# Sixteen distances between the experts' weights and the operands they meet, one for each expert and inner block

## The chip, the cores and the metric

The kernel runs on one core of one Trainium2 chip, in one launch. The metric is device microseconds. The kernel before was timed in 3 runs: median 689.16 us, lowest 688.44, highest 694.27.

## What is computed

Three layers follow each other. An attention over 2 batches of 8 heads (576 positions, head dimension 64) adds a banded softmax and a softmax over positions averaged by four. Its output is read as x with 1152 rows of 512. Then:

```python
h = x @ w_in                                  # 512 -> 2048
x = (h * (1.0 / (1.0 + np.exp(-h)))) @ w_out  # 2048 -> 512

p = domain_probs / (domain_probs.sum(-1, keepdims=True) + 1e-09)
out = np.zeros((N, D), dtype=np.float32)
for e in range(E):                            # 4 experts, 512 -> 1024 -> 512
    h = np.maximum(x @ w1[e], 0.0)
    out += p[:, e:e + 1] * (h @ w2[e])
```

All is float32. The change touches the place in memory of w1 and w2 alone.

## The kernel before

**Split products.** A float32 operand of the two feed-forward layers is held as a high part and a low part (float32r), and each product is three matmuls: high by high, high by low, low by high (`mm3`, line 493, and `prod`, line 692). In a matmul one operand is stationary (128 columns are loaded into the array by a weight load of its own, PEld in the profile) and the other is moving (256, 320 or 384 columns are streamed through).

**Stages of the experts.** For each expert `e` (4), each chunk of rows `ci` (0 to 2 of 256 rows, 3 of 384) and each inner block `k` (4) there is one stage. `first_products` (line 646) makes 24 matmuls at line 495: w1 stationary, x moving, 256 columns, or 384 in chunk 3. `second_products` (line 703) makes 21 matmuls at line 699: the activations `h` stationary, w2 moving, 256 columns; in chunk 3 another 12 with the tiles `o`, 33 in all. The second products of a stage come after the first products of the next one. This makes 3,072 matmuls for the experts, 192 for each pair of an expert and an inner block in each of the two products: 96 first ones (72 of 256 columns and 24 of 384) and 96 second ones.

**Where the operands lie.** In the built program `xh` and `xl` begin at byte 128 modulo 512 in every partition, `wbuf` at 192, `wext` (and `u5`) at 448, the tiles `h` and `o` at 384. Slices of them begin at multiples of 512 from there, but for the two row chunks of the first feed-forward pass that start at rows 576 and 832 (256 more, modulo 512). "Distance" is here the first byte of the moving operand minus that of the stationary one, modulo 512, which gives before:

| products | moving | stationary | distance |
|---|---|---|---|
| experts, first | `xh`, `xl` | w1 in `wbuf` | 448 |
| experts, second, k = 0, 1 | w2 in `wext` | `h`, `o` | 64 |
| experts, second, k = 2, 3 | w2 in `wbuf` | `h`, `o` | 320 |
| feed-forward, weights in `wext`, `u5` | `xh`, `xl` | w_in | 192 |

**Refilling.** While chunk 3 of an expert runs, the next expert's weights are split into the same places: `split_u` (line 601; ACT writes the high part at line 608, POOL or DVE the low part at line 610) and `split_kk` (line 614; lines 624 and 626). The raw weights come by DMA from SP's queue (line 583) well before. The tile framework makes a write wait for the matmuls that still read the bytes it overwrites, and its scheduler sets each engine's order by the priorities of the ticks (`at_prio`).

Of the kernel before, what the change touches and what calls it, by code (L numbers as in the profile page):

```python
# [9 lines left out]
F32 = mybir.dt.float32  # L10
F32R = mybir.dt.float32r
# [4 lines left out]
ACTF = mybir.ActivationFunctionType  # L16
ALU = mybir.AluOpType
# [16 lines left out]
UW = 2048  # L34
NE = 4
KF = 7 * 256
# [20 lines left out]
STAGE = 4  # L57
EXPERT = 72


@with_exitstack
def attention_moe_kernel(ctx, tc, kqa, kqb, qtl, va, vb, w64, w1d, w2d, dpr, out):
    nc = tc.nc
    PE, ACT, DVE, POOL, SP = nc.tensor, nc.scalar, nc.vector, nc.gpsimd, nc.sync

    const = ctx.enter_context(tc.tile_pool(name="const", bufs=1))
# [22 lines left out]
    xl = const.tile([128, HP, NT], F32R, name="xl")  # L89
    acc = const.tile([128, 9 * 512], F32, name="acc")  # L90
    const.tile([128, 16], F32, name="gap")
    wbuf = const.tile([128, 8 * UW], F32R, name="wbuf")
    const.tile([128, 16], F32, name="gap_w")
    prt = const.tile([128, 9, NE + 1], F32, name="pr")
    pr, prs = prt[:, :, 0:NE], prt[:, :, NE:NE + 1]
# [26 lines left out]
    def follow(i, earlier, reason):  # L122
        tc.add_manual_dep(i.ins, earlier.ins.name, mybir.DependencyInfo(mybir.DependencyClass.NoSync, mybir.DependencyReason.DATA),
                          reason=reason)

    def behind(eng, i):
        if eng in latest:
            follow(i, latest[eng], "background work")
        return i
# [7 lines left out]
    unit = {}  # L137
    wext = []
# [3 lines left out]
    def slot(u):  # L142
        s = SLOT[u] if u < 8 else (2, 3)[u % 2]
        if s == 5:
            wext.append(u5_p[0].enter_context(tc.tile_pool(name="u5", bufs=1)).tile([128, 2 * UW], F32R, name="u5"))
        t, o = (wext[s - 4], 0) if s > 3 else (wbuf, 2 * UW * s)
        return t[:, o:o + UW], t[:, o + UW:o + 2 * UW]
# [23 lines left out]
    def split_piece():  # L171
        u, j, t = loaded.popleft()
        with at_prio(needed(u, j) - LEAD_SPLIT):
            split_raw(u, j, t)
        held[0] -= 1
        load_piece()

    def split_raw(u, j, t):
        if j == 0:
            unit[u] = slot(u)  # L180
        h, l = unit[u]
        if u < 8:
            c = slice(j * 512, (j + 1) * 512)
            v = t.bitcast(I32).rearrange("p (n t) -> p n t", t=2)
            a = d_p.tile([128, 512], F32, tag="dec", name="dec")
            ai = a.bitcast(I32)

            top = t.bitcast(U16).rearrange("p (n t) -> p n t", t=4)[:, :, 1]
            ACT.activation(out=a, in_=v[:, :, 1].bitcast(F32), func=ACTF.Copy, scale=2.0 ** -112)
            ACT.activation(out=v[:, :, 0], in_=top, func=ACTF.Copy, scale=2.0 ** -13, bias=2.0 ** -14 - 0.5)  # L190
            i = DVE.scalar_tensor_tensor(out=ai, in0=ai, scalar=3, in1=v[:, :, 0],  # L191
                                         op0=ALU.logical_shift_left, op1=ALU.bitwise_or)
            if u in behind_job:
                follow(i, behind_job[u], "first weights")
            DVE.scalar_tensor_tensor(out=ai, in0=v[:, :, 1], scalar=-2 ** 31, in1=ai,  # L195
                                     op0=ALU.bitwise_and, op1=ALU.bitwise_or)
            ACT.activation(out=h[:, c], in_=a, func=ACTF.Copy)  # L197
            POOL.tensor_tensor(out=l[:, c], in0=a, in1=h[:, c].bitcast(F32), op=ALU.subtract)  # L198
        else:
            c = slice(j * 1024, (j + 1) * 1024)  # L200
            behind(ACT, ACT.activation(out=h[:, c], in_=t, func=ACTF.Copy))
            behind(DVE, DVE.tensor_tensor(out=l[:, c], in0=t, in1=h[:, c].bitcast(F32), op=ALU.subtract))


    actx = ExitStack()
# [279 lines left out]
    def attn_tick():  # L485
        for _, _, f, args in sorted(plan.pop(tick[0], ()), key=lambda e: e[:2]):
            prio(tick[0] - (0 if f in main_parts else LEAD_ATTN))
            f(*args)
        tick[0] += 1
        prio(tick[0])  # L490
# [66 lines left out]
    wk, w1k = {}, {}  # L557

    def tick_of(e, ci, k):
        return 96 + EXPERT * e + STAGE * (4 * ci + k) + (2 * k if ci == 3 else 0)  # L560
# [12 lines left out]
    def stage_ahead():  # L573
        while todo and not pieces:
            i = next((i for i, p in enumerate(stg_pools) if held[i] < 3), None)
            if i is None:
                break
            held[i] += 1
            e, x, k = todo.popleft()
            t = stg_pools[i].tile([128, 1024], F32, tag="stg", name="kst")  # L580
            staged[e, x, k] = (t, i)
            with at_prio(need_of(e, x, k) - LEAD_KLOAD):
                SP.dma_start(out=t.rearrange("p (s c) -> p s c", c=256) if x == "k" else t,
                             in_=w2d[e, k] if x == "k" else w1d[e, :, 1024 * k:1024 * k + 1024])
# [10 lines left out]
                                (c[:, 0], t[:, 2], c[:, 2]), (c[:, 1], t[:, 1], c[:, 0])):  # L595
                    behind(eng, eng.tensor_tensor(out=o, in0=a, in1=b, op=ALU.subtract))

    def home_u(k):
        h, l = slot(8 + k // 2)
        c = slice(1024 * (k % 2), 1024 * (k % 2) + 1024)  # L600
        return h[:, c], l[:, c]

    def split_u(e, k):
        t, i = staged.pop((e, "u", k))
        h, l = w1k[k] = home_u(k)
        for c in (slice(0, 512), slice(512, 1024)):
            with at_prio(tick_of(e, 0, k) - LEAD_USPLIT):
                ACT.activation(out=h[:, c], in_=t[:, c], func=ACTF.Copy)
                eng = POOL if k in U_LO_POOL else DVE
                eng.tensor_tensor(out=l[:, c], in0=t[:, c], in1=h[:, c].bitcast(F32), op=ALU.subtract)  # L610
        held[i] -= 1
        stage_ahead()

    def split_kk(e, k):
        t, i = staged.pop((e, "k", k))
        t = t.rearrange("p (s c) -> p s c", c=256)
        c = sums.pop((e, "k", k))
        b, o = (wext[0], 2 * KF * k) if k < 2 else (wbuf, 2 * UW * (k - 2))
        h = b[:, o:o + KF].rearrange("p (s c) -> p s c", c=256)
        l = b[:, o + KF:o + 2 * KF].rearrange("p (s c) -> p s c", c=256)  # L620
        parts = (slice(2, 4), slice(4, 6), slice(0, 2), slice(6, 7))
        for part, (r, x) in enumerate(zip(parts, (t[:, 0:2], t[:, 2:4], c[:, 0:2], c[:, 2:3]))):
            with at_prio(tick_of(e, 0, k) + 6 - LEAD_KSPLIT):
                a = ACT.activation(out=h[:, r], in_=x, func=ACTF.Copy)  # L624
                eng = POOL if (k, part) in LO_ON_POOL else DVE
                b = eng.tensor_tensor(out=l[:, r], in0=x, in1=h[:, r].bitcast(F32), op=ALU.subtract)  # L626
                if e == 0 and k > 1:
                    behind(ACT, a)
                    behind(eng, b)
        wk[k] = (h, l)  # L630
        held[i] -= 1
        stage_ahead()
# [165 lines left out]
    def close_attn():  # L798
        while plan:
            attn_tick()  # L800
        actx.close()
        late = ctx.enter_context(tc.tile_pool(name="late", bufs=1))
        wext.append(late.tile([128, 4 * KF], F32R, name="wext"))
        u5_p.append(ExitStack())
        pp_p.append(ctx.enter_context(tc.tile_pool(name="pp", bufs=1, space=PSUM)))

# [6 lines left out]
    for hf in range(2):  # L813
        u0 = 4 * hf
        dt = 48 / (12 * len(CHUNKS[hf]))
        for ci, (o, n) in enumerate(CHUNKS[hf]):
# [15 lines left out]
            if hf == 0 and ci == 2:  # L832
                close_attn()
                limit[0] = 6
            if hf == 1 and lastc:
                u5_p[0].close()
                ks_p.append(ctx.enter_context(tc.tile_pool(name="ks", bufs=2)))
                stage_ahead()
                for k in range(4):
                    sum_ahead(0, k)  # L840
                    if k < 2:
                        split_kk(0, k)
# [26 lines left out]
    for k in range(2, 4):  # L869
        split_kk(0, k)  # L870
    for k in range(4):
        w1k[k] = home_u(k)

    class Chunk:
        pass
# [1 line left out]
    def finish(st, ch, p):  # L877
        e, ci, k = st.at
        prio(p)
        second_products(st, ch)  # L880
        if ci == 3 and e < NE - 1:
            split_kk(e + 1, k)
            if k < 2:
                sum_ahead(e + 1, k + 2)
        if k == 3:
            outputs(e, ci, ch, p)

    before = None
    for e in range(NE):
        for ci in range(4):  # L890
            ch = Chunk()
            for k in range(4):
                st = Stage()
                st.at = (e, ci, k)
                first_products(st)
                if ci == 3 and e < NE - 1:
                    split_u(e + 1, k)
                if ci == 2 and k % 2 == 0 and e < NE - 1:
                    sum_ahead(e + 1, k // 2)
                if before:  # L900
                    finish(*before, tick_of(e, ci, k) + (3 if ci == 3 else 2))
                before = (st, ch)
# [57 lines left out]
```

## Time and profile before

| | us |
|---|---|
| median of 3 runs | 689.16 |
| lowest and highest run | 688.44, 694.27 |
| profiled execution, first to last instruction (span) | 693.6 |
| TensorE matmul busy | 659.5 (95%) |
| VectorE, ScalarE, GpSimd busy | 440.3, 332.0, 247.5 |

The profile lists no time of its own for the profiled execution beside its span. Busy time of PE is the union of its matmuls, which overlap in the pipeline: a matmul of 256 columns is shown with some 280 ns although the next one starts 113 to 118 ns later. The pace, start to start, is therefore read from how many matmuls fill a stretch.

### The profile page before, as it was taken

Reading aid. Unit: us, or ns where it says so; the run is one execution under the profiler, and the core shown is the slowest. Engines: PE = TensorE matmul, PEld = TensorE weight load, DVE = VectorE, ACT = ScalarE, POOL = GpSimd, SP = SyncE. Lnnn points to the kernel's source line nnn. Section 1 sums busy time; section 2 is a strip of 40 time slices with the busy share of each in tenths; the row PEclk is TensorE's granted clock in tenths of the full one; section 3 lists DMA queues with packets and bytes.
Section 4 is the critical chain, followed back from the end, with each engine's and each line's share of the span. In section 5 each row is a group of like instructions: output and inputs, shape, how many; then the busy total and the mean of one; then the engine's idle time right before and its main releaser. Section 6 shows DMA issues by size and latency. Waiting matters only on the chain.

```text
span 693.6 us, 13797 instructions
## 1 busy us (share of the span) xinstructions
PE 659.5 (95%) x5516; PEld 641.9 (93%) x5516; DVE 440.3 (63%) x882; ACT 332.0 (48%) x753; POOL 247.5 (36%) x346
## 2 busy tenths in 40 slices
PE   4779779999999999999999999999999999999996
PEld 3659669999999999999999999999999999999996
DVE  4678967638664643675665985548855669756444
ACT  4559766647653532544335643345533356433321
POOL 4344762114240000344264432456232654322210
PEclk9597989999999999999999999999999999999999
DMA  8665663105250210042001420004300010000001
GB/s 248 215 183 166 184 176 96 34 1 161 92 174 1 81 44 1 1 144 70 1 1 48 136 61 1 1 2 122 93 31 1 1 60 3 1 32 17 17 31 45
DMA packets 16927, 48.16 MB, mean 69 GB/s; under 512 B 2976, under 2 KB 4256, under 8 KB 16864
## 3 DMA queue, kind: packets, MB, share of 16 engines
q1 hardware_dynamic: 16864, 47.29, 22.0%
q8 instruction: 43, 0.70, 0.4%
q14 instruction: 20, 0.16, 0.1%
HBM read 44.93 MB, written 2.36 MB: 68 GB/s over the span
## 4 chain that ended last, share of the span: by engine, by line
PE 83%; DMA 6%; DVE 6%; ACT 2%; issue 2%; POOL 1%; SPq 0%; ACTq 0%; DVEq 0%; POOLq 0%
PE mm L495 53%; PE p L699 26%; DMA stg<-in_w_dram 3%; DMA vg<-in_va_dram 2%; DVE dec L191 1%; DVE dec L195 1%; DVE gl L521 1%; PE s L328 1%; PE o L420 1%; PE t L388 1%; PE o L416 1%; DVE acc L727 1%; DVE gf L515 0%; POOL vg L265 0%; PE s L352 0%
## 5 line engine op out<-in xcount | busy, mean ns | idle before, releaser
L495 PE MATMUL mm<-xh,wbuf 128*128 128x256 f32 (+2 forms) x1280 | 268.7, 296 | 3.4 <-ACT xh L432 2.6
L495 PEld LDWEIGHTS mm<-xh,wbuf 128*128 128x128 f32 x1280 | 211.0, 190 | 4.7 <-ACT xh L432 3.0
L495 PE MATMUL mm<-xl,wbuf 128*128 128x256 f32 (+2 forms) x640 | 189.8, 297 | 0.0
L681 POOL TENSOR_TENSOR r<-r 128x128 f32<-128x128 f32 x160 | 93.5, 597 | 183.2 <-ACT r L675 143.7
L684 DVE TENSOR_TENSOR h<-r,h 128x384 fp32r<-128x384 f32 (+1 forms) x128 | 91.4, 717 | 64.6 <-ACT h L683 64.4
L495 PEld LDWEIGHTS mm<-xl,wbuf 128*128 128x128 f32 x640 | 121.6, 190 | 0.1
L683 ACT ACTIVATE h<-r 128x384 fp32r<-128x384 f32 (+1 forms) x128 | 73.2, 577 | 85.3 <-POOL r L681 54.1
L495 PE MATMUL mm<-gh,wbuf 128*128 128x256 f32 (+2 forms) x512 | 106.0, 300 | 6.4 <-ACT wbuf L197 3.5
L699 PE MATMUL p<-wext,h 128*128 128x256 f32 x672 | 91.5, 279 | 0.0
L495 PEld LDWEIGHTS mm<-gh,wbuf 128*128 128x128 f32 x512 | 83.8, 191 | 8.0 <-ACT wbuf L197 3.7
L699 PE MATMUL p<-wbuf,h 128*128 128x256 f32 x672 | 84.5, 278 | 0.0
L699 PEld LDWEIGHTS p<-wext,h 128*128 128x128 f32 x672 | 84.4, 188 | 0.0
L699 PEld LDWEIGHTS p<-wbuf,h 128*128 128x128 f32 x672 | 81.2, 188 | 0.0
L495 PE MATMUL mm<-gl,wbuf 128*128 128x256 f32 (+2 forms) x256 | 74.7, 296 | 0.5 <-DVE gl L521 0.5
L675 ACT ACTIVATE r<-mm 128x512 f32<-128x512 f32 x48 | 28.7, 597 | 75.5 <-PE mm L495 75.1
L681 DVE TENSOR_TENSOR r<-r 128x128 f32<-128x128 f32 x96 | 33.5, 349 | 37.7 <-ACT r L675 33.0
L495 PEld LDWEIGHTS mm<-gl,wbuf 128*128 128x128 f32 x256 | 48.6, 190 | 0.8 <-DVE gl L521 0.8
L521 DVE TENSOR_TENSOR gl<-gf,gh 128x256 fp32r<-128x256 f32 (+2 forms) x64 | 34.8, 547 | 18.0 <-ACT gh L520 15.4
L198 POOL TENSOR_TENSOR wbuf<-dec,wbuf 128x512 fp32r<-128x512 f32 x24 | 32.5, 1360 | 31.1 <-ACT wbuf L197 20.2
L727 DVE SCALAR_TENSOR_TENSOR acc<-p,pr,acc 128x256 f32<-128x256 f32 (+1 forms) x63 | 36.1, 605 | 5.9 <-PE p L699 5.9
L626 POOL TENSOR_TENSOR wext<-kst,wext 128x512 fp32r<-128x512 f32 x8 | 10.7, 1344 | 78.4 <-ACT wext L624 42.9
L515 DVE SCALAR_TENSOR_TENSOR gf<-th,mm 128x256 f32<-128x256 f32 (+2 forms) x64 | 28.4, 449 | 15.3 <-ACT th L514 13.6
(122 smaller groups left out, 980.2 us busy)
## 6 DMA issues: line engine op xcount, KB each, us to landing
stg<-in_w_dram SPq DMA_DIRECT2D x32, 512.0 KB, 4.3
kst<-in_w2d_dram SPq DMA_DIRECT2D x16, 512.0 KB, 3.6
kst<-in_w1d_dram SPq DMA_DIRECT2D x12, 512.0 KB, 3.6
kq<-in_kqa_dram SPq DMA_DIRECT2D x8, 419.0 KB, 3.3
kq<-in_kqb_dram SPq DMA_DIRECT2D x8, 323.0 KB, 10.8
vg<-in_va_dram SPq DMA_DIRECT2D x8, 288.0 KB
stg<-in_w1d_dram SPq DMA_DIRECT2D x4, 512.0 KB
vw<-in_vb_dram SPq DMA_DIRECT2D x8, 180.0 KB
```

Source lines behind the costliest of these rows:

```text
L191: i = DVE.scalar_tensor_tensor(out=ai, in0=ai, scalar=3, in1=v[:, :, 0], op0=ALU.logical_shift_left, op1=ALU.bitwise_or)
L198: POOL.tensor_tensor(out=l[:, c], in0=a, in1=h[:, c].bitcast(F32), op=ALU.subtract)
L495: ins = [PE.matmul(out=ps, lhsT=l, rhs=r, start=(first and i == 0), stop=(last and i == n - 1)) for i, (l, r) in enumerate(pairs)]
L515: DVE.scalar_tensor_tensor(out=gf[:, 0:n], in0=th[:, 0:n], scalar=1.0, in1=ps[:, 0:n], op0=ALU.add, op1=ALU.mult)
L521: latest[DVE] = DVE.tensor_tensor(out=gl[ft][:, 0:n], in0=gf[:, 0:n], in1=gh[ft][:, 0:n].bitcast(F32), op=ALU.subtract)
L626: b = eng.tensor_tensor(out=l[:, r], in0=x, in1=h[:, r].bitcast(F32), op=ALU.subtract)
L675: ACT.activation(out=r[:, 0:4].rearrange("p s t -> p (s t)"), in_=ps[:, 0:512], func=ACTF.Relu)
L681: latest[eng] = eng.tensor_tensor(out=r[:, o], in0=r[:, a], in1=r[:, b], op=op)
L683: ACT.activation(out=h, in_=r[:, part], func=ACTF.Copy)
L684: latest[DVE] = DVE.tensor_tensor(out=l, in0=r[:, part], in1=h.bitcast(F32), op=ALU.subtract)
L699: ins = [PE.matmul(out=ps, lhsT=x, rhs=y, start=(opens and k == 0 and i == 0), stop=(k == 3 and i == n - 1), skip_group_check=True) for i, ...
L727: DVE.scalar_tensor_tensor(out=o, in0=ps, scalar=p, in1=o, op0=ALU.mult, op1=ALU.add)
```

## The change

The first weights `w1` of each expert and inner block are moved by a number of bytes that gives their first products one of 16 distances, and `w2` likewise for the second products (`GAPS`, picked by `ROW_W1` and `ROW_W2`). `home_u` now lays the high and low halves of one inner block side by side with 128 floats to spare, `split_raw` uses `home_u` for the first expert's w1, and `wbuf` and `wext` grow by 2048 and 1024 bytes, both multiples of 512. Each value stands once in each table; the distances are now:

| expert | first products, k = 0 to 3 | second products, k = 0 to 3 |
|---|---|---|
| 0 | 448, 0, 256, 64 | 320, 64, 448, 0 |
| 1 | 480, 32, 320, 96 | 32, 464, 128, 384 |
| 2 | 464, 16, 384, 128 | 496, 256, 48, 96 |
| 3 | 496, 48, 416, 192 | 192, 416, 16, 480 |

```diff
+GAPS = (0, 16, 32, 48, 64, 96, 128, 192, 256, 320, 384, 416, 448, 464, 480, 496)
+ROW_W1 = ((12, 0, 8, 4), (14, 2, 9, 5), (13, 1, 10, 6), (15, 3, 11, 7))
+ROW_W2 = ((9, 4, 12, 0), (2, 13, 6, 10), (15, 8, 3, 5), (7, 11, 1, 14))
...
-    wbuf = const.tile([128, 8 * UW], F32R, name="wbuf")
+    wbuf = const.tile([128, 8 * UW + 512], F32R, name="wbuf")
...
     def split_raw(u, j, t):
-        if j == 0:
+        if j == 0 and u < 8:
             unit[u] = slot(u)
-        h, l = unit[u]
         if u < 8:
+            h, l = unit[u]
...
         else:
-            c = slice(j * 1024, (j + 1) * 1024)
-            behind(ACT, ACT.activation(out=h[:, c], in_=t, func=ACTF.Copy))
-            behind(DVE, DVE.tensor_tensor(out=l[:, c], in0=t, in1=h[:, c].bitcast(F32), op=ALU.subtract))
+            h, l = home_u(0, 2 * (u - 8) + j)
+            behind(ACT, ACT.activation(out=h, in_=t, func=ACTF.Copy))
+            behind(DVE, DVE.tensor_tensor(out=l, in0=t, in1=h.bitcast(F32), op=ALU.subtract))
...
-    def home_u(k):
-        h, l = slot(8 + k // 2)
-        c = slice(1024 * (k % 2), 1024 * (k % 2) + 1024)
-        return h[:, c], l[:, c]
+    def home_u(e, k):
+        o = 4 * UW + 2176 * k + (448 - GAPS[ROW_W1[e][k]]) % 512 // 4
+        return wbuf[:, o:o + 1024], wbuf[:, o + 1024:o + 2048]
...
-        h, l = w1k[k] = home_u(k)
+        h, l = w1k[k] = home_u(e, k)
...
-        b, o = (wext[0], 2 * KF * k) if k < 2 else (wbuf, 2 * UW * (k - 2))
+        b, o, d = (wext[0], (2 * KF + 128) * k, 64) if k < 2 else (wbuf, 2 * UW * (k - 2), 320)
+        o += (GAPS[ROW_W2[e][k]] - d) % 512 // 4
...
-        wext.append(late.tile([128, 4 * KF], F32R, name="wext"))
+        wext.append(late.tile([128, 4 * KF + 256], F32R, name="wext"))
...
-        w1k[k] = home_u(k)
+        w1k[k] = home_u(0, k)
```

No instruction is added or taken away. Because the new place of a weight overlaps the old one by a shift, some writes wait for other matmuls, and the scheduler moves a few rows. On ScalarE, where expert 1's first weights of inner block 0 are written during chunk 3 of expert 0 (`wbuf<-kst`; `h_4500` and `h_4558` are the activations of two neighbouring stages), the order before is

```order
L683 ACTIVATE h_4500<-r 128x512
L608 ACTIVATE wbuf<-kst 128x512
L667 ACTIVATE r<-mm 128x256
L671 ACTIVATE o_4560<-mm 128x128
L608 ACTIVATE wbuf<-kst 128x512
L667 ACTIVATE r<-mm 128x256
L671 ACTIVATE o_4560<-mm 128x128
```

and now

```order
L687 ACTIVATE h_4500<-r 128x512
L671 ACTIVATE r<-mm 128x256
L675 ACTIVATE o_4560<-mm 128x128
L611 ACTIVATE wbuf<-kst 128x512 x2
L671 ACTIVATE r<-mm 128x256
L675 ACTIVATE o_4560<-mm 128x128
```

The first of the two writes of weights has moved behind the two reads of the first half's result (lines are 3 or 4 higher in the changed kernel). The same engine, where expert 1's second weights of inner block 2 are written (`wbuf<-kst` and `wbuf<-ks`), before

```order
L683 ACTIVATE h_4843<-r 128x384
L624 ACTIVATE wbuf<-kst 128x512
L624 ACTIVATE wbuf<-ks 128x256
L683 ACTIVATE h_4843<-r 128x512
L624 ACTIVATE wbuf<-ks 128x512
L624 ACTIVATE wbuf<-kst 128x512
```

and now

```order
L687 ACTIVATE h_4843<-r 128x384
L628 ACTIVATE wbuf<-kst 128x512
L687 ACTIVATE h_4843<-r 128x512
L628 ACTIVATE wbuf<-ks 128x256
L628 ACTIVATE wbuf<-ks 128x512
L628 ACTIVATE wbuf<-kst 128x512
```

The activations' second part stands one row earlier, ahead of the second write of weights.

## Rows read from the trace of the kernel before

**Rows 1.** The page: busy us, share of the span, instructions of each engine.

```profile
PE 659.5 (95%) x5516; PEld 641.9 (93%) x5516; DVE 440.3 (63%) x882; ACT 332.0 (48%) x753; POOL 247.5 (36%) x346
```

**Rows 2.** Stretches, PE alone: from:to us, length, PE busy (matmuls), granted clock, DMA.

```profile
0.00:150.00 150.00, 123.92 (x1278) 0.89 0.51 151
150.00:306.66 156.66, 155.31 (x1167) 1.00 0.21 68
306.66:680.90 374.24, 374.24 (x3024) 1.00 0.12 38
680.90:693.60 12.70, 6.02 (x52) 0.92 0.17 62
```

**Rows 3.** Groups by line and shape from 306.66 us: busy us, mean ns, idle before.

```profile
L495 PE MATMUL mm<-xh,wbuf 128*128 128x256 f32 x768 | 143.7, 279 | 0.0
L699 PE MATMUL p<-wext,h 128*128 128x256 f32 x672 | 91.5, 279 | 0.0
L699 PE MATMUL p<-wbuf,h 128*128 128x256 f32 x672 | 84.5, 278 | 0.0
L495 PE MATMUL mm<-xh,wbuf 128*128 128x384 f32 x256 | 68.2, 337 | 0.0
L495 PE MATMUL mm<-xl,wbuf 128*128 128x384 f32 x128 | 43.1, 337 | 0.0
```

**Rows 4.** The chain of waits, pieces: start us, us, engine, tile, line, matmuls.

```profile
338.35 2.47 PE p L699 x21
340.82 2.73 PE mm L495 x24
...
366.91 4.24 PE mm L495 x24
371.14 2.47 PE p L699 x21
373.61 4.19 PE mm L495 x24
...
397.89 2.74 PE mm L495 x24
400.63 3.74 PE p L699 x33
404.37 2.83 PE mm L495 x24
407.20 0.59 PE p L699 x5
...
411.77 2.38 PE p L699 x21
...
417.68 2.47 PE p L699 x21
420.15 2.73 PE mm L495 x24
422.89 2.38 PE p L699 x21
```

**Rows 5.** Stretches of the first feed-forward pass and after, columns as in rows 2.

```profile
250.77:262.08 11.31, 11.31 (x99) 1.00 0.01 1
273.38:290.02 16.64, 16.64 (x98) 1.00 0.00 0
306.66:315.50 8.84, 8.84 (x79) 1.00 0.72 256
```

**Rows 6.** Timeline of PE: start us, us, engine (PEld: weight load), line, tiles, count.

```profile
422.50 0.19 PEld L495 LDWEIGHTS mm<-xh,wbuf 128*128 128x128 f32 x1
422.61 0.28 PE L495 MATMUL mm<-xh,wbuf 128*128 128x256 f32 x1
422.61 0.64 PEld L699 LDWEIGHTS p<-wbuf,h 128*128 128x128 f32 x5
```

**Rows 7.** Timeline of ScalarE in chunk 3 of expert 0, columns as in rows 6.

```profile
368.89 0.63 ACT L608 ACTIVATE wbuf<-kst 128x512 fp32r<-128x512 f32 x1 [1.63 <-PE mm L495]
...
380.31 0.63 ACT L624 ACTIVATE wext<-kst 128x512 fp32r<-128x512 f32 x1 [1.17 <-PE p L699]
```

**Rows 8.** Timeline of PE in the attention: four transposes.

```profile
114.79 0.60 PE L388 MATMUL t<-ident,sm 128*70 128x128 f32 x4
```

**Rows 9.** The line of these transposes: duration ns min/median/max, first and last start.

```profile
L388 PE MATMUL t<-ident,sm x72: 271/273/428, 20.5 to 143.7; 128*70 128x128 f32 x72
```

## Prediction

> **What bounds the kernel now.** I read the page first: PE is busy for 659.5 of 693.6 us, every other engine for 63% or less [rows 1]. Then the stretches: PE loses time before 150 us, but from 306.66 to 680.90 us, where the experts run, it is busy for all of 374.24 us at a granted clock of 1.00, which is 2.4 GHz, and the DMA share is 0.12 [rows 2]. The groups of that stretch show 0.0 us of idle time ahead of PE's matmuls [rows 3]. So nothing but the pace of the matmuls sets the time of the experts, and a change of where their operands lie can act only through that pace, or by making a wait where there is none.
>
> The pace is read from the chain of waits, which lists whole blocks [rows 4]. Blocks of 256 columns run at one of two paces. Fast: 2.38 us for 21 or 3.74 us for 33, which is 113.3 ns. Slow: 2.83 us for 24 or 2.47 us for 21, some 117.8 ns; the step between them is 4.4 ns. A block of 24 that begins slow and turns fast takes 2.73 us. Both paces stand at each distance that the experts have: at 448 (404.37 slow, 420.15 fast after its first two), at 64 (338.35 slow, 411.77 fast) and at 320 (417.68 slow, 422.89 fast). With 384 columns blocks take 4.24 or 4.19 us for 24, or 176.7 and 174.6 ns [rows 4].
>
> One more distance is seen, 192, in the first feed-forward pass: 96 matmuls in 11.31 us, 117.8 ns, slow throughout, while 96 of 384 columns at 192 take 16.64 us, 173.3 ns, which is a fast pace that the experts' 384-column blocks at 448 do not reach [rows 5]. In the same rows 78 matmuls of 256 columns at 448 take 8.84 us, 113.3 ns.
>
> The mix, with the 384 matmuls of 384 columns at the mean of their two values (175.6 ns) costing 67.4 us: the other 2,640 of the 3,024 rows of the stretch take 374.24 - 67.4 = 306.8 us, or 116.2 ns each. At 113.3 ns (and 173.3) everywhere the stretch would be 2,640 x 2.9 = 7.7 plus 384 x 2.3 = 0.9, together 8.6 us shorter; at 117.8 (and 177.8, one step above 173.3) 4.2 + 0.8 = 5.0 us longer.
>
> **The change part by part.**
>
> *Distances.* Of the 16 values, 64, 192, 320 and 448 are known. They are a quarter of the work: each value has 192 matmuls, 168 of 256 columns and 24 of 384. The other twelve values carry 12 x 168 = 2,016 and 12 x 24 = 288 matmuls, and no steady stretch of before shows any of them. All four known values are 64 modulo 128, so they say little of values near 0 modulo 128. Bounds from the nearest rows: below, the fast pace for all twelve, 2,016 x 2.9 + 288 x 2.3 = 6.5 us less. Above, far away, a weight load that does not overlap the running matmul at all: the load at 422.50 starts 110 ns before the matmul that uses it [rows 6], and with that on top of the pace the two blocks at distance 0 alone, 192 matmuls, would cost 21 us, all twelve values 250 us. I see nothing that points near that end: single meetings at other distances are already in the trace and cost nothing. When second products in `wbuf` give way to first products, the last stream (byte 192 modulo 512) runs beside a weight load at distance 0; when they lie in `wext` (448) it is at distance 256. The block that follows takes 2.73 us for 24 in both cases (420.15 after 0, 340.82 after 256) [rows 4]. And the transposes of the attention, whose stationary operand steps by 280 bytes, pass four distances in a row at an even (0.60 - 0.27) / 3 = 0.11 us [rows 8, 9]. So I take the two known paces for the twelve new values. Their mix is open: the experts' mix is 116.2 ns, and the only other known distance, 192, stood at 117.8. I take the middle, 117.0: 2,016 x 0.8 = 1.6 us more, and nothing for the 384-column blocks, where 448 and 192 differ the other way.
>
> The rows show a stream and a load running together at two paces whose cause they don't name. By the Trainium skill (TensorE: Matmul & The Clock Gate, Part 2, the step on LDWEIGHTS) the array reads the two operands through two independent ports, and loading the next weights takes no read bandwidth from the running matmul. By that rule the distance would not matter, the sum would have no term for it and the time would stay; it is a rival below. The two paces at one distance agree with it; that 192 was never fast with 256 columns does not speak for it. No run here shows a steady stretch that decides it.
>
> *Waits.* The shifted places overlap the old ones, so some writes of new weights wait longer. Expert 1's first weights of block 0 move up by 480 bytes, 120 floats; the first 512 columns of the new copy then reach into the old second half, whose first three matmuls must be over: 3 x 176.7 = 0.53 us later than at 368.89 [rows 4, 7]. They are used in the block at 397.89, 29 us later. Second weights start to be written at 380.31 and move by up to six matmuls of 117.8 ns, 0.7 us; they are used from 407.20 [rows 4, 7]. More than 20 us cover less than 1 us, so both cost nothing, and without that cover they would cost 0.5 to 0.7 us per write. The write that waits longer is queued behind the two reads of the first half's result and no longer ahead of them, so ScalarE does not hold them up; in the other place shown, the activations' second part comes one write (0.63 us [rows 7]) earlier. The second write still waits for the same last matmul. SP's queue and the DMAs keep their order, and `wbuf` and `wext` grow by multiples of 512, so nothing else changes its distance. Cost: 0.
>
> *Sum.* +1.6 us. The profiled execution, 693.6 us, would become 695.2. It lies 4.4 us above the median of the runs, 689.16, and near the highest, 694.27. I apply the difference to the median, since the stretch before 150 us, which the change does not touch, can move runs by itself (clock 0.89 there [rows 2]): 690.8, about 691 us.
>
> **The rivals.**
>
> 1. *The forecast*, two paces in another mix: 691, between 684 and 694 by the bounds above (12 of 16 values all fast: -5 us with some left slow, or all slow: +5). For it: both paces at every distance within the experts. Against: the known four are a narrow sample. Chance 0.45.
> 2. *The change does nothing*: the mix hangs on the order of blocks, not on the distance. In the rows the pace turns after second products while the distances stay the same (417.68 slow to 420.15 fast, 400.63 fast to 404.37 slow) [rows 4]. Then 689, within 2 us. Chance 0.14.
> 3. *A third, slower pace near distance 0*, which is the other side. Mechanism: a matmul and the weight load for the next one start together, within 0.01 us (422.61 for both) [rows 6], and near distance 0 at the same byte modulo 512, so they meet at the start of every matmul and not once in passing. An estimate from the step of the rows: one more step of 4.4 ns, 122.2 ns. With the seven values within 48 of 0 (0, 16, 32, 48, 464, 480, 496): 7 x 192 x 6.0 = 8.1 us, 697. If it repeats every 128 bytes, all twelve new values: 12 x 192 x 6.0 = 13.8 us, 703. It decides from about a further 5 ns on seven values. For it: 64, 192, 320, 448 all lie as far from multiples of 128 as can be, and a single meeting at distance 0 need not show what a steady one does. Against: that meeting and the transposes. Chance 0.31.
> 4. *The fast pace prevails*: most new values lock fast as 448 did for 78 matmuls [rows 5]. 689.2 - 6.5 = 683 us, with the known four fast too 680.6. Chance 0.10.
>
> **How the numbers follow.** About 1% (7 us) is what a measurement of this kernel can tell from no change. Slower by over 1% (above 696): rival 3 but for its mildest form, 0.31. Faster by over 1% (below 682.3): the far half of rival 4 and a little of the forecast's, 0.08. Within 1%: the rest, 0.61. The predicted time is that of the likeliest case, 691. The forecast's own range is 684 to 694; the range that holds 8 in 10 also takes in rival 3 up to its repeated form and most of rival 4: 682 to 704.
>
> **What would show it.** Right: PE still without a wait from 306 us on, an expert stretch of some 376 us, and blocks of 24, 21 and 33 at 2.72 to 2.83, 2.38 to 2.47 and 3.74 to 3.89 us whatever their distance. Rival 2: the same pieces of the chain to 0.01 us in the same places. Rival 3: blocks of 21 at 2.57 us or more in the places with distances near 0, expert 0's first products of block 1 and second products of block 3 above all. Rival 4: hardly a 2.83. What would make it wrong altogether: a wait for `wbuf` or `wext` ahead of line 499 or 703, or a pace above 125 ns in many blocks.

## The result, and the profile after

The changed kernel takes 694.55 us (median of 12 runs, 689.63 to 698.28), the kernel before, timed again beside it, 689.67 us (12 runs, 688.04 to 694.27). The ratio is 1.0058 with a 95% interval of 1.0031 to 1.0086: 2.1 to 5.9 us slower, and the middle, 4.0 us, is two and a half times the forecast's 1.6 (the two medians lie 4.9 us apart).

The stretches (from:to us, length, busy time of PE, PEld, VectorE, ScalarE and GpSimd with their instructions, granted clock, DMA share, GB/s), cut as in [rows 2]; the third has PE alone, again begins with the experts' first matmul and holds 3,024 matmuls.

```profile
0.00:150.00 150.00, 123.66 (x1294) 108.40 (x1295) 101.75 (x248) 91.29 (x246) 62.49 (x101) 0.91 0.50 151
150.00:304.60 154.60, 153.45 (x1152) 151.71 (x1151) 92.24 (x168) 78.76 (x171) 34.90 (x30) 1.00 0.22 69
...
304.60:683.31 378.71, 378.71 (x3024) 1.00 0.12 37
```

That stretch grew from 374.24 to 378.71 us with the same clock and the same number of matmuls, and PE is busy for all of it. From the first to the last of all 3,072 starts it is 379.98 us before and 384.45 us after, 4.47 us more. The experts begin 2.06 us earlier here; this start lies between 298.6 and 306.7 us in the runs below, changed or not, so one run's whole time says little, and from here on this stretch (384.45 us, "expert stretch") is what is compared.

No wait has come: no engine is listed as waited for by PE between 304.60 and 690 us, and the groups that answer to [rows 3] (busy us, mean ns of one, idle time before) still have no idle time.

```profile
L499 PE MATMUL mm<-xh,wbuf 128*128 128x256 f32 x768 | 146.0, 281 | 0.0
...
L703 PE MATMUL p<-wext,h 128*128 128x256 f32 x672 | 92.0, 280 | 0.0
L703 PE MATMUL p<-wbuf,h 128*128 128x256 f32 x672 | 86.1, 281 | 0.0
...
L499 PE MATMUL mm<-xh,wbuf 128*128 128x384 f32 x256 | 68.0, 336 | 0.0
...
L499 PE MATMUL mm<-xl,wbuf 128*128 128x384 f32 x128 | 43.0, 336 | 0.0
```

What changed is the pace, the time from one matmul's start to the next one's. Pieces of the chain of waits of the changed kernel (start us, us, what, matmuls), to be held against [rows 4]:

```profile
326.34 2.52 PE p L703 x21
328.86 3.36 PE mm L499 x28
...
337.08 2.48 PE p L703 x21
339.56 2.83 PE mm L499 x24
342.38 2.40 PE p L703 x21
344.78 2.83 PE mm L499 x24
347.61 2.52 PE p L703 x21
...
376.86 3.88 PE p L703 x33
...
396.85 2.85 PE mm L499 x24
399.69 3.96 PE p L703 x33
...
435.52 2.88 PE mm L499 x24
...
649.39 2.73 PE mm L499 x24
```

The blocks at 326.34, 347.61 and 399.69 are second products at distance 0: 2.52 us for 21 and 3.96 us for 33 are 120.0 ns each, a pace that no row of before has. The first 24 of the 28 at 328.86 are also at 0, and the 24 at 435.52, at distance 96, take the same 120.0 ns. The blocks at 64 (337.08, 339.56) and 448 (342.38, 344.78) run at the two known paces, slow or turning from slow to fast, and the one at 649.39, at 192, is fast for all but its first steps. The one at 396.85 is at 480, with 118.6 ns from start to start, which is neither.

From start to start of each matmul in the trace, sorted by the distance of its operands (mean ns; 72 first products of 256 columns, 24 of 384, and 96 second products each):

| distance | first, 256 | first, 384 | second, 256 |
|---|---|---|---|
| 0 | 120.00 | 173.58 | 119.76 |
| 16 | 118.74 | 176.54 | 117.36 |
| 32 | 116.79 | 173.38 | 117.71 |
| 48 | 116.90 | 173.83 | 118.25 |
| 64 | 117.43 | 173.50 | 117.66 |
| 96 | 119.88 | 176.50 | 119.79 |
| 128 | 118.82 | 176.04 | 118.70 |
| 192 | 113.99 | 174.42 | 116.58 |
| 256 | 119.79 | 173.83 | 119.64 |
| 320 | 117.10 | 174.12 | 117.12 |
| 384 | 118.49 | 175.62 | 119.38 |
| 416 | 118.65 | 176.54 | 118.02 |
| 448 | 117.56 | 173.12 | 116.27 |
| 464 | 119.42 | 173.42 | 118.02 |
| 480 | 118.46 | 174.00 | 118.23 |
| 496 | 118.17 | 173.88 | 117.72 |

The whole loss can be counted from it. The twelve new values have 2,015 steps of 256 columns with a mean of 118.60 ns; before, the mean over all was 116.31: 4.6 us more. The four known values went from 116.31 to 116.74 in 672 steps, 0.3 us more, and the 384 steps of 384 columns from 175.67 to 174.52 on the mean, 0.4 us less. Together 4.5 us, the 4.47 us measured.

### The profile page after: what moved, and what is told of

Same layout as the page of the kernel before. It is cut to its first block, busy times and chain, and to the rows that moved or that the text cites. A ratio compares the mean times of both kernels' runs of the same rounds, so it can differ in the third digit from the quotient of the medians.

```text
span 696.0 us, 13806 instructions
## 1 busy us (share of the span) xinstructions
PE 661.8 (95%) x5516; PEld 644.6 (93%) x5516; DVE 443.5 (64%) x882; ACT 331.6 (48%) x753; POOL 247.8 (36%) x346
## 4 chain that ended last, share of the span: by engine, by line
PE 79%; DMA 8%; DVE 6%; ACT 2%; issue 2%; POOL 2%; SPq 0%; ACTq 0%; DVEq 0%; POOLq 0%
PE mm L499 50%; PE p L703 26%; DMA stg<-in_w_dram 6%; DMA vg<-in_va_dram 2%; DVE dec L199 1%; DVE dec L195 1%; DVE gl L525 1%; PE s L332 1%; PE t L392 1%; ACT stg L194 1%; PE o L424 1%; PE o L420 1%; DVE acc L731 1%; ACT dec L193 1%; POOL vg L269 0%
## 5 line engine op out<-in xcount | busy, mean ns | idle before, releaser
L703 PE MATMUL p<-wbuf,h 128*128 128x256 f32 x672 | 86.1, 281 | 0.0
L703 PEld LDWEIGHTS p<-wbuf,h 128*128 128x128 f32 x672 | 82.6, 189 | 0.0
L685 DVE TENSOR_TENSOR r<-r 128x128 f32<-128x128 f32 x96 | 36.4, 380 | 38.5 <-ACT r L679 33.9
```

Source lines behind the costliest of these rows:

```text
L685: latest[eng] = eng.tensor_tensor(out=r[:, o], in0=r[:, a], in1=r[:, b], op=op)
L703: ins = [PE.matmul(out=ps, lhsT=x, rhs=y, start=(opens and k == 0 and i == 0), stop=(k == 3 and i == n - 1), skip_group_check=True) for i, ...
```

## The experiments

Each kernel is the changed one with other numbers in its tables (written short in the diffs), so each has the same instructions. The tables move the weights alone; x and `h` stay in their places. The number that decides is the expert stretch of one profiled execution of each; before has 379.98 us, the change 384.45 us. Theory A in the texts says that a meeting's own distance sets its pace; B that the new layout and its waits cost the time; C that the neighbouring blocks do.

**same_layout**: the new layout, but the distances of before.

```diff
-ROW_W1 = ((12, 0, 8, 4), (14, 2, 9, 5), (13, 1, 10, 6), (15, 3, 11, 7))
-ROW_W2 = ((9, 4, 12, 0), (2, 13, 6, 10), (15, 8, 3, 5), (7, 11, 1, 14))
+ROW_W1 = ((12, 12, 12, 12), ) * 4
+ROW_W2 = ((4, 4, 9, 9), ) * 4
```

> The changed kernel's new places and spare floats, but with the distances of before (448 for the first products, 64 and 320 for the second). The stretch from the first to the last of the 3,072 expert matmuls took 379.98 us before and 384.45 us after. Theory A, the distance sets the pace: 380.0 us within 0.5. Rival B, the layout or its waits cost the time: about 384.

380.34 us. The chain's pieces are those of before again, 2.47, 2.73 and 2.38 us:

```profile
330.63 2.47 PE p L703 x21
333.11 2.73 PE mm L499 x24
335.84 2.38 PE p L703 x21
338.22 2.83 PE mm L499 x24
```

The layout is out: it costs 0.4 us at most. The waits of the change are not in this run, though. With one distance for all experts a weight comes back to its predecessor's very place, and ScalarE writes it as before, ahead of the two reads and waiting for PE as long:

```profile
361.17 0.63 ACT L611 ACTIVATE wbuf<-kst 128x512 fp32r<-128x512 f32 x1 [1.63 <-PE mm L499]
```

What puts them out is the trace of the changed kernel, in which PE waits for nothing in this stretch. So B is out by the two together, and the 4 us come from the distances.

**all_0**: distance 0 everywhere.

```diff
+ROW_W1 = ((0, 0, 0, 0), ) * 4
+ROW_W2 = ((0, 0, 0, 0), ) * 4
```

> All blocks at distance 0. Theory A (each distance has a pace of its own, whatever its neighbours): 256-column matmuls at 120.0 ns and 384-column ones at 173.6 as in the changed kernel's blocks at 0, so 1,152 x 120.0 + 1,536 x 119.8 + 384 x 173.6 = 388.9 us for the expert stretch. Rival C (the time comes from neighbouring blocks lying at different distances, which one distance for all takes away): 380 us or less.

388.88 us; the run took 702.68 us, before on the same chip 695.74 (one run each). Every block of 256 columns, first or second product, stands at 120.0 ns:

```profile
337.71 2.52 PE p L703 x21
340.23 2.88 PE mm L499 x24
343.11 2.52 PE p L703 x21
345.63 2.88 PE mm L499 x24
```

So 120.0 ns belongs to distance 0 and needs no neighbour of another kind, and C's 380 us or less is out. Neither this run nor same_layout has shifted writes, so between the two the distances alone cost 8.5 us: 2,687 steps by 3.47 ns are 9.3 us, less 0.8 us for the 384-column blocks (173.61 ns for 175.67).

**all_192** and **all_448**: one known distance everywhere, 7 and 12 in the tables.

```diff
+ROW_W1 = ROW_W2 = ((7, 7, 7, 7), ) * 4
```

> All blocks at distance 192. Theory A: first products at 114.0, second at 116.6 (or 114.3 as in chunk 3) and 174.4 ns for 384 columns, as in the changed kernel's blocks at 192: 377 us (or 374). Rival C: 380 us, as any distance for all. Third possibility, the slow pace of 117.8 ns that 192 has in the first feed-forward pass: 1,152 and 1,536 at 117.8 and 173.3 for 384 columns, 383 us.

> All blocks at distance 448. Theory A: 117.6, 116.3 and 173.1 ns as in the changed kernel's blocks at 448: 380.5 us. Rival C: 380 us. It tells apart whether the distances that are 64 modulo 128 keep two paces when all blocks share one of them: one pace throughout would be 371 us (113.3) or 383 us (117.8).

380.22 and 380.53 us. For 192 both numbers of A were missed: I had held one of the paces to belong to it, and it has both. C's 380 us lies near both runs, but its reason, any one distance for all, fell with all_0. The pieces of all_192:

```profile
333.39 2.40 PE p L703 x21
335.79 2.83 PE mm L499 x24
338.62 2.40 PE p L703 x21
341.02 2.83 PE mm L499 x24
...
384.73 4.16 PE mm L499 x24
388.90 3.89 PE p L703 x33
392.79 2.73 PE mm L499 x24
395.52 3.89 PE p L703 x33
```

Fast and slow blocks take turns, though every matmul has the same distance: second products fast after slow first ones (from their fourth or fifth matmul on), the next first ones slow. all_448 does the same. At these two distances the pace is a state that the entry into a new block turns over.

**w1_only** and **w2_only**: the change's table for one kind of weight, the distances of before for the other.

```diff
 w1_only:
+ROW_W2 = ((4, 4, 9, 9), ) * 4
 w2_only:
+ROW_W1 = ((12, 12, 12, 12), ) * 4
```

> The first weights at the 16 distances of the change, the second ones at 64 and 320 as before. Theory A (each product pays for its own distance): the first products cost 203.1 us of pace in the changed kernel against 201.2 before, so the expert stretch goes from 380.0 to 381.9 us. Rival C (cost comes from changes of distance between neighbouring blocks): most of the 4.5 us stays, 383 to 384.5, since nearly every boundary still joins two different distances.

> The second weights at the 16 distances of the change, the first ones at 448 as before. Theory A: the second products cost 181.3 us against 178.8, so 380.0 + 2.5 = 382.5 us for the expert stretch. Rival C: 383 to 384.5 us.

383.39 and 382.17 us, 3.4 and 2.2 us over before. A's sum was 1.5 us short for w1_only, which lies in C's band, and met w2_only to 0.3 us, below that band. The halves add up to 5.6 us, not 4.5, so part of the pace does depend on what runs next to it: in w1_only the untouched second products, at 64 and 320, slowed to 117.22 and 117.33 ns (116.85 and 116.14 before), and first products at 192 took 117.9 ns for 114.0 in the change. Of the new values those at 0 (119.97) and 256 (119.78) did not move; first products at 16, 32, 384 and 464 did, by 1.1 to 1.2 ns either way (16 from 118.74 to 117.57, 32 from 116.79 to 118.01).

**other_places**: the same sixteen values, dealt to other experts.

```diff
+ROW_W1 = ((15, 3, 11, 7), (13, 1, 10, 6), (14, 2, 9, 5), (12, 0, 8, 4))
+ROW_W2 = ((2, 13, 6, 10), (15, 8, 3, 5), (7, 11, 1, 14), (9, 4, 12, 0))
```

> The same 16 distances once each, but the experts' rows of the first table reversed and those of the second turned by one, so that every block has other neighbours. Theory A: the same mean pace for each distance within 1 ns, except for 64, 192, 320 and 448, which have two paces (113.3 and 117.8 ns); expert stretch 384.5 within 1.5 us. Rival C: paces of single distances change by several ns, as their neighbours do.

384.43 us, as the change. The edit does less than the text above says: expert 3 here has both rows that expert 0 has in the change, and expert 1 both rows of expert 2, so half of the blocks keep their neighbours. Their paces say how well a trace repeats: for values that are not 64 modulo 128 the 256-column means agree with the change's within 0.2 ns (first products at 0 119.96, at 16 118.78). The other two experts are the test. Their 256-column means at such values agree within 0.6 ns (first products at 96 119.92, at 32 116.49; second ones at 128 118.62, at 416 117.49). With w1_only the pace of a new value goes with its distance to 1.2 ns, and at 0, 96, 128 and 256 to 0.4. The 384-column means at 32, 48 and 416, which do have other neighbours, changed by 1.7 to 3.2 ns, so theirs does not.

**delta_256** and **delta_128**: first and second products at two different values of the good class, 256 or 128 apart.

```diff
 delta_256:
+ROW_W1 = ((12, 12, 12, 12), (7, 7, 7, 7), (4, 4, 4, 4), (9, 9, 9, 9))
+ROW_W2 = ((7, 7, 7, 7), (12, 12, 12, 12), (9, 9, 9, 9), (4, 4, 4, 4))
 delta_128:
+ROW_W1 = ((4, 4, 4, 4), (7, 7, 7, 7), (9, 9, 9, 9), (7, 7, 7, 7))
+ROW_W2 = ((7, 7, 7, 7), (4, 4, 4, 4), (7, 7, 7, 7), (9, 9, 9, 9))
```

> Only distances that are 64 modulo 128, first and second products 256 apart: 448 with 192, 192 with 448, 64 with 320, 320 with 64, one pair for each expert. Theory D: these four distances have the same two paces and what chooses is the step between neighbouring blocks: 448 with 64 or 320 (before) turns the pace once in a stage, equal distances (192 with 192, 448 with 448) twice. If a step of 256 never turns it, an expert runs at one pace throughout, 113.3 ns (92.8 us for an expert) or 117.8 (95.9 us); if it turns like the others, 94.9 to 95.2 us for each. Rival: the four distances differ from each other whatever stands beside them, and the four experts differ.

> Only distances that are 64 modulo 128, first and second products 128 apart as before but with other values: 64 with 192, 192 with 64, 320 with 192, 192 with 320, one pair for each expert. Theory D (the step between the two distances chooses the paces, not their values): as before, blocks of 384 columns at 174.6 and 176.7 ns in turn and 95.0 us for each expert within 0.2, stretch 380.0 us. Rival: equal or 256-apart distances gave 173.4 ns at 384 columns because of their values; then 384 columns run at 173.4 in those experts whose first products lie at 192.

381.49 us, with 95.08, 95.23, 95.55 and 95.64 us for the four experts: the two with 192 and 448 turn, the two with 64 and 320 alone stay slow (117.3 to 117.7 ns on the mean; one block of 24 is fast). So the step does not choose alone, as D has it: at the same step of 256 the values decide. delta_128 gives 379.92 us and 95.03, 95.11, 94.85 and 94.93 us, as expected for 256 columns. Its 384-column blocks do not: 173.7 ns at 64 and 320, 175.7 ns at 192, the reverse of the rival's forecast. Nor is it the value alone, since 192 has 173.4 ns in all_192; beside second products at 64 or 320 it has 175.7. A block at 64 between second products at 192, and one at 192 between second products at 64:

```profile
370.29 4.17 PE mm L499 x24
...
473.34 4.24 PE mm L499 x24
```

**fine**: sixteen values a few floats apart, around 20 to 76 and near 192 and 448.

```diff
+GAPS = (20, 24, 36, 40, 52, 56, 60, 68, 72, 76, 184, 188, 196, 200, 440, 456)
```

> Sixteen other distances in the same places: 52, 56, 60, 68, 72 and 76, 184, 188, 196, 200, 440 and 456 (within 12 bytes of 64, 192 and 448), and 20, 24, 36 and 40. Theory E, the pace changes in steps of 16 bytes or more: the twelve keep the two paces 113.3 and 117.8 ns (means 114 to 117.8) and the four run at 116.5 to 119 like 16, 32 and 48; expert stretch 381 to 383 us. Rival F, every 4 bytes count: the twelve show cycles of their own like 48 and 464 (single steps from 113 to 123 ns), stretch 383 to 386 us. A distance at 113.3 ns in all of its blocks would be the one to use everywhere.

387.70 us, above the bands of both theories, 381 to 383 (E) and 383 to 386 (F); the one run took 702.31 us, before on that chip 694.95. Pieces at second products at 196 (322.86), 20 (327.44) and 52 (338.17), first at 52 (340.70, and 390.66 with 384 columns):

```profile
322.86 2.54 PE p L703 x21
...
327.44 2.57 PE p L703 x21
...
338.17 2.52 PE p L703 x21
340.70 2.94 PE mm L499 x24
...
390.66 4.29 PE mm L499 x24
```

Of its 32 means with 256 columns (first and second products at 16 values) half are over 119.5 ns and two under 117 (first products at 56 with 116.9, second ones at 60 with 116.6). Four bytes above 192, second products take 120.53 ns on the mean, against 113.3 or 117.8 for a steady block at 192; at 52 first products take 121.7 ns, and 178.7 ns with 384 columns; the highest mean is 121.9 ns, of second products at 20. Neither band foresaw that a few bytes count so much; which offsets are bad follows no order that I can see in these sixteen.

**all_64**: 64 everywhere.

```diff
+ROW_W1 = ROW_W2 = ((4, 4, 4, 4), ) * 4
```

> All blocks at distance 64. Theory G, read from the runs so far: going into a block at 64 or 320 (64 modulo 256) keeps the pace, going into one at 192 or 448 (192 modulo 256) turns it; only the stage whose first and second products are mixed can change it otherwise. So one pace for whole chunks: slow, as in the two such experts of the run with distances 256 apart (95.6 us each), 382.5 us for the expert stretch and 0.4% above before; or fast, 371 to 374 us. Theory A alone (own mix of each distance): 380.5 us.

382.99 us, slow throughout, the slow case of G (382.5), in which 64 keeps the pace it is entered with. Timed beside it: 692.61 us (12 runs), before 689.57 (23 runs), ratio 1.0035, interval 1.0007 to 1.0063. Its pieces beside those of all_192 show the difference, 2.47 us for 2.40:

```profile
333.30 2.47 PE p L703 x21
335.77 2.83 PE mm L499 x24
338.60 2.47 PE p L703 x21
341.07 2.83 PE mm L499 x24
```

**one_turn**: 64 everywhere, but for one block of second products at 192 per chunk, which should turn the slow pace into the fast one and leave it there.

```diff
+ROW_W1 = ((4, 4, 4, 4), ) * 4
+ROW_W2 = ((4, 7, 4, 4), ) * 4
```

> All blocks at distance 64 but the second products of inner block 1, which come right after the mixed stage of each chunk and lie at 192. Theory G: if the mixed stage ends slow, that one turn makes the five blocks behind it fast: some 139 of the 180 matmuls of a chunk of 256 rows at 113.3 ns, in chunk 3 only the 384-column blocks at 173.6, so 376 us for the expert stretch, 0.6% below before. If the mixed stage keeps the pace, chunks are fast and slow in turn: 380 us. Rival (the turn has nothing to do with distance): 382.5 us, as with 64 throughout.

380.45 us, not the 376 that the theory gave. That its other case, chunks fast and slow in turn, has 380 is chance: the chunks do not take turns.

```profile
330.85 2.40 PE p L703 x21
333.24 2.72 PE mm L499 x24
335.96 2.38 PE p L703 x21
338.35 2.83 PE mm L499 x24
341.17 2.47 PE p L703 x21
```

The turn comes as forecast in nine of the twelve chunks of 256 rows, these pieces among them: the block at 192 (330.85) goes fast, the next two at 64 stay fast (113.4 and 113.6 ns). In the first chunk of experts 1 to 3 those two are slow (117.8 and 117.9 ns), which no theory here foresaw. Where the turn comes, the first products of the next chunk (338.35) are slow again, and all behind them up to its own block at 192: half of the theory fell, since 64 does not always keep the fast pace. Timed beside before: 690.16 us (12 runs), ratio 1.0009, interval 0.9988 to 1.0030. Of the two versions timed so, then, neither beats the kernel before.

## Why the prediction was right or wrong

**That PE's pace alone decides** held: PE is without a wait from 304.60 us on, and the clock is 1.00 there as before.

**The waits** cost nothing, as forecast; how long they are was met for one write by chance and missed for the other. ScalarE writes expert 1's first weights in the changed kernel so (start us, us, what):

```profile
368.15 0.38 ACT L671 ACTIVATE r<-mm 128x256 f32<-128x256 f32 x1 [1.68 <-PE mm L499]
368.43 0.27 ACT L675 ACTIVATE o<-mm 128x128 fp32r<-128x128 f32 x1
368.59 0.64 ACT L611 ACTIVATE wbuf<-kst 128x512 fp32r<-128x512 f32 x1
...
379.99 0.63 ACT L687 ACTIVATE h<-r 128x512 fp32r<-128x512 f32 x1 [1.78 <-POOL r L685]
380.53 0.62 ACT L628 ACTIVATE wext<-kst 128x512 fp32r<-128x512 f32 x1
```

The block of matmuls that they stand in began at 366.04, so the write comes 2.55 us into it; before, it was 368.89 - 366.91 = 1.98 us [rows 4, 7]. That is 0.57 us later for the 0.53 forecast. But the forecast had it wait for three matmuls, and the profile lists no wait ahead of it: it starts right behind the two reads (368.15, 368.43) that now stand before it. The second weights' write comes 380.53 - 376.86 = 3.67 us into its block of second products, before 380.31 - (373.61 + 4.19) = 2.51 us [rows 4, 7]: 1.16 us later, where 0.7 was the most foreseen. It too has no wait listed; it now stands behind the activations' second part (379.99), which came after it before. PE waits for neither.

**The failed step** is "So I take the two known paces for the twelve new values", at 117.0 ns. They have paces of their own. At 0 every step inside a block is 120 ns, and 256 averages 119.6 to 119.9. At others a cycle repeats (96 steps between 115 and 125 ns, some stretches at 464 between 116 and 130), with means from 116.8 to 119.9. The mean is 118.60, 2.3 ns over the mean of before and not 0.8: the term of 1.6 us was 4.6. It lies above even the slower known pace, 117.8, which the forecast's own range has as its worst case. The direction was right, the size a third of it, and the direction was luck: it came from taking the middle of two known paces, and neither is what most of the new values have. Two terms left at nothing, the known four (0.3 us more) and the 384 columns (0.4 us less), almost cancel. The sentence that failed with it is that single meetings cost nothing: the meeting where one block gives way to another is one step of 24, and the transposes of [rows 8, 9] are three steps of 0.11 us at three distances, with 128 columns. Neither could show a steady pace. The forecast's own range, 684 to 694, does not hold the 694.55 us; the wider one, 682 to 704, does, because it takes in rival 3.

**What should have shown the forecast**, blocks of 21 at 2.38 to 2.47 us whatever the distance and a stretch of 376 us, did not come: 2.52 us at distance 0, and 378.71 us.

**Rival 3**, the slower pace near 0, was half right. Distance 0 has one, but 120.0 ns, 3.7 ns over the mean of before where the rival had 6.0, under its mark of 2.57 us for 21. And it is not nearness to 0: the seven first products within 48 bytes of it average 118.4 ns, the other five new ones (96, 128, 256, 384, 416) 119.1. By the paces its repeated form, every 128 bytes, was nearer, with 2.3 ns for 6.0.

**Rival 2**, no effect of the distance, is refuted by all_0 beside same_layout. With it falls the conclusion drawn from the Trainium skill (TensorE: Matmul & The Clock Gate, Part 2, the step on LDWEIGHTS): if the operands come through independent ports and a weight load takes nothing from the running matmul, the distance should not matter, and the measured 8.5 us between two kernels that differ in distances alone say that it does. The measurement decides. What that rival said of the blocks' order is true of the four known values: there the pace is a state that entering a block keeps or turns (all_192). At the new ones other neighbours moved a mean of the change by 1.2 ns at most. **Rival 4**, the fast pace everywhere, has nothing for it: of the twelve new values none has a mean under 116.7 ns in the changed kernel.

**Still open**: why a pace depends on the distance. That the stream and the next weight load meet in the memory is my guess, and no run takes one of them away. Open too is whether it is the distance or the places. No single operand's place is the whole of it: x lies at byte 128 modulo 512 in all first products, whose means go from 114.0 to 120.0 ns, and `h` at 384 in all second ones, with 116.3 to 119.8. But no run moved both operands by the same bytes, which would leave the distance as it is. And open is what decides between the two paces at 64 and 320: in one_turn the first products at 64 handed the fast pace on to second products at 64, and these did not hand it on to the next first ones at 64. The rules given for it were read from the traces after the fact, and one_turn, the run made to try them, bore out half, and that not in every chunk.

## What to carry to other kernels

When PE never waits, the place of its operands modulo 512 bytes can still be a cost: look at the start-to-start pace of whole blocks, and try first the distances that did best here (64 modulo 128: 113.3 or 117.8 ns for 256 columns, against 120.0 at 0). A single meeting of two operands in an old trace tells nothing of a steady pace; a run with one distance everywhere is a short edit and does, or shows that the distance has two (all_192). Compare the stretch in question from trace to trace, since the rest of a run can move the whole time by more than the effect.

## What the runs showed of the hardware that was not expected

- Matmuls of 256 columns in float32r go steadily at 113.3, 117.8 or 120.0 ns, start to start, at a granted clock of 1.00, or through repeating cycles with means of 116.5 to 121.9 ns. Where the weights lie modulo 512 bytes, told here by their distance from the other operand, is part of what picks it: 119.7 to 120.0 at 0 with any neighbours that were tried, 119.6 to 119.9 at 256.
- At 64, 192, 320 and 448 two paces stand side by side. Entering a block at 192 or 448 mostly turns the pace; at 64 the slow pace stays for the whole expert part (all_64).
- An offset of 4 bytes counts: second products at 196 take 120.5 ns, those at 192 in a steady block 113.3 or 117.8.
- With 384 columns distance 0, the worst of the change's values with 256 columns, is among the best (173.6 ns; the lowest mean is 173.1, at 448); the worst seen is 178.7 at 52.
